# T in two tiles of long runs, an unsigned read, a moved weight piece and turns on the sync queue: the prologue of a Fourier and SoLU kernel

## The chip, the cores and the metric

The kernel runs on one core of one Trainium2 chip. The metric is the device time of one execution in microseconds. "Span" is the length of the profiled execution; the device time is some 2 us longer.

## The reference

```python
X = np.fft.fft(x, axis=1)                 # x: (8, 3136, 256) float32
X = np.fft.fft(X, axis=2).real            # -> (25088, 256) tokens
h = X @ w_in                              # w_in (256, 1024)
e = np.exp(h - h.max(-1, keepdims=True))
solu = h * (e / (e.sum(-1, keepdims=True) + 1e-9))
ln = (solu - mean(solu)) / sqrt(var(solu) + 1e-6) * g_ln
return ln @ w_out                         # w_out (1024, 256)
```

The weights come as 64-bit floats, in two 32-bit words each, and the kernel makes float32 of them.

## The kernel before

The sequence transform is done in two factors. The first (F) runs chunk by chunk and its results go out to a DRAM tile `zd`; a **turn** reads them back with another order of axes (`g`); the second factor is a product with the table `T`, one per **unit** of 128 rows, and there are 100 units in four pairs. Each unit then goes through `up` (the product with w_in, TensorE), `even` and `join` (VectorE), `expo` (ScalarE), `product` (VectorE), a mean (GpSimd), `square` (ScalarE) and, four steps later, `down` (the product with w_out). `ev`, which `even` writes, is the first VectorE step of a unit, and serves below as the mark of where a unit stands.

```python
T = const.tile([P, NK, P], FP32, name="T")

def turn(pr, i, engines=(nc.gpsimd,) * 4):               # four transfers of 160 KB
    pr.g[i] = gpool.tile([P, KG, D], FP32, tag="g", name="g")
    for j in range(4):
        engines[j].dma_start(out=pr.g[i][j * NH : (j + 1) * NH, :, :], in_=zd[j, :, i * KG : (i + 1) * KG, :])

def spread(t):                                           # r: one row of q across partitions
    nc.sync.dma_start(out=t.r, in_=t.q[0:1, P : 2 * P])

def load_table(self):                                    # T, two loads of 400 KB, runs of 256 B
    for b in range(2):
        r = slice(b * N2, (b + 1) * N2)
        nc.sync.dma_start(out=T[r, :, r], in_=t_tab)

# narrow(): two 32-bit words to one float32
bits(lo, lo, 1, ALU.logical_shift_right)
m = lo.bitcast(FP32)
nc.vector.scalar_tensor_tensor(out=m, in0=lo, scalar=2.0 ** -31, in1=mantissa, op0=ALU.mult, op1=ALU.add)

def centre(self):                                        # takes the mean of w_out's rows off
    for c in range(KF):
        nc.tensor.matmul(cs, ones, Wo[:, c, :], start=(c == 0), stop=(c == KF - 1))
    nc.scalar.mul(out=wbar, in_=cs, mul=1.0 / FF)
    nc.vector.tensor_tensor(out=Wo, in0=Wo, in1=wbar...., op=ALU.subtract)

# ... chunks of the first pair; w_out and T are loaded behind chunk 3 ...
turn(first, 0, (nc.sync, nc.gpsimd) * 2)
...                                                      # narrow_out(0..3)
for i in range(len(units) + lag):                        # the train, one unit a step
    ...
    even(cur, up(cur, 0)); odd = up(cur, 1)
    take2(nxt, transform2(pairs[nxt.p], nxt.k1)); spread(nxt)
    ...
    join(cur, odd); ...; expo(cur); ...
    for s in cur.signs: product(cur, s)                  # GpSimd's mean (nmean) right behind each
    if i == 0: weights.centre()
    for s in cur.signs: square(cur, s)
    ...
    if 0 < i + 1 < NK // KG: turn(first, i + 1)          # turns 1 to 4, by GpSimd
    if ahd: ahead(ahd, cur.k1)                           # loads and gathers of the next pair
```

## Time and profile before

| | before |
|---|---|
| device time, median of 3 | 1192.98 us (1190.93 to 1195.39) |
| span of the profiled run | 1189.9 us |
| ev of units 0, 1, 2, 3 | 63.15, 71.33, 78.19, 87.04 us |
| first matmul of unit 5's `up` | 101.25 us |
| last ScalarE scaling starts | 1186.42 us, 3.48 us ahead of the end |

Units 0 to 4 are the start; behind them TensorE is full, and each unit takes 11.65 us. What the start wins or loses moves everything behind it.

These are the rows of the program's last line (engine, operation, count, then shortest, median and longest duration in ns, and the first and last time), and below it the waits of the sync engine from 1160 us on (total, times, longest us):

```profile
L722 POOLq DRAIN  x3: 46/102/3455, 1183.5 to 1189.6; - x3
```

### The profile page before, as it was taken

To read this page: it belongs to the slowest core of one execution; us is meant where nothing else is said; L and a number is where in the kernel's file an instruction comes from. 1 tells how busy PE (TensorE), PEld (TensorE's weight loads), DVE (VectorE), ACT (ScalarE), POOL (GpSimd) and SP (SyncE) were. 2 spreads that over 40 slices of the span, in tenths; PEclk is the share of its full clock that TensorE was granted. 3 is DMA by queue.
4 is the path that set the end of the run, shared out by engine and by line. 5 is a ranking of instruction groups with operands and counts; after the bars stand their busy time and mean duration, and the time that the engine had idled before them with its cause. 6 is when DMAs were issued, how large, how long until landed. Compare 5 with 4: busy or idle time off the path is not lost. (4 is left out here: it accounts for less than half of the span.)

```text
span 1189.9 us, 15918 instructions
## 1 busy us (share of the span) xinstructions
PE 1154.2 (97%) x4720; PEld 875.9 (74%) x4720; DVE 907.9 (76%) x1241; ACT 679.0 (57%) x1404; POOL 496.9 (42%) x964
## 2 busy tenths in 40 slices
PE   2889999999999999999999999999999999999998
PEld 1556777777777777777777777777777777777787
DVE  8879777777768877787778878777786887877780
ACT  4557655655546656565555656565555555655561
POOL 3045444443544443432544453433453344333433
PEclk9999999999999999999999999999999999999999
DMA  9873765756775765654775776664684453544534
GB/s 246 206 187 72 190 162 152 200 140 163 171 172 160 187 172 155 167 144 131 172 187 159 176 177 154 158 181 122 150 198 131 109 152 100 145 111 120 142 92 117
DMA packets 460886, 185.39 MB, mean 156 GB/s; under 512 B 428854, under 2 KB 442750, under 8 KB 460800
## 3 DMA queue, kind: packets, MB, share of 16 engines
q1 hardware_dynamic: 446848, 145.63, 48.6%
q0 software_dynamic: 13952, 38.75, 11.9%
q8 instruction: 38, 0.62, 0.2%
q14 instruction: 48, 0.39, 0.1%
HBM read 44.78 MB, written 38.80 MB: 70 GB/s over the span
## 5 line engine op out<-in xcount | busy, mean ns | idle before, releaser
L323 PE MATMUL ps_o<-Wo,uT 128*128 128x256 f32 x3136 | 693.4, 379 | 0.3 <-ACT ot L328 0.3
L323 PEld LDWEIGHTS ps_o<-Wo,uT 128*128 128x128 f32 x3136 | 611.0, 196 | 62.8 <-issue 0.9
L222 PE MATMUL ps_h<-Wi,q 128*128 128x512 f32 x800 | 362.3, 595 | 0.1
L254 DVE SCALAR_TENSOR_TENSOR u<-h,u 128x1024 f32<-128x1024 f32 x196 | 240.1, 1225 | 57.0 <-ACT u L246 31.1
L236 DVE CUSTOM_DVE_ANT_0 h<-ev,ps_h 128x1024 f32<-128x1024 f32 x196 | 231.8, 1219 | 50.3 <-PE ps_h L222 41.3
L256 POOL TENSOR_SCALAR nmean<-usum 128x1 f32<-128x1 f32 x196 | 80.4, 411 | 445.7 <-DVE u L254 445.5
L222 PEld LDWEIGHTS ps_h<-Wi,q 128*128 128x128 f32 x800 | 152.7, 191 | 149.8 <-issue 144.6
L263 ACT ACTIVATE h<-u,nmean 128x1024 f32<-128x1024 f32 x196 | 225.0, 1149 | 61.3 <-POOL nmean L256 60.0
L228 DVE SCALAR_TENSOR_TENSOR ev<-w_mid,r,ps_h 128x1024 f32<-128x1024 f32 x100 | 127.8, 1278 | 133.1 <-PE ps_h L222 126.2
L246 ACT ACTIVATE u<-h,neg 128x1024 f32<-128x1024 f32 x196 | 225.4, 1150 | 6.5
L291 DVE STREAM_TRANSPOSE v<-u 128x1024 f32<-128x1024 f32 x192 | 228.6, 1236 | 0.1
L200 ACT COPY q<-ps 128x256 f32<-128x256 f32 x100 | 37.2, 372 | 289.3 <-PE ps L194 263.0
L328 ACT ACTIVATE ot<-ps_o,rs 128x256 f32<-128x256 f32 x196 | 87.0, 462 | 61.3 <-PE ps_o L323 55.2
L335 POOL DMA_INDIRECT out_dram<-ot,idx x96 | 103.0, 1073 | 35.4 <-issue 20.7
L194 PEld LDWEIGHTS ps<-T,g 128*128 128x128 f32 x400 | 60.9, 194 | 52.1 <-issue 50.9
L169 PE MATMUL ps<-y,F 98*100 98x258 f32 (+3 forms) x288 | 72.2, 387 | 22.2 <-DVE y L122 22.2
L278 POOL TENSOR_TENSOR rs<-v,neg_half 128x2 f32<-128x2 f32 (+1 forms) x100 | 84.2, 842 | 7.8
L244 ACT ACTIVATE neg<-nmax 128x1 f32<-128x1 f32 x196 | 38.3, 195 | 61.0 <-DVE nmax L236 60.2
L169 PEld LDWEIGHTS ps<-y,F 98*100 98x100 f32 x288 | 46.0, 179 | 34.6 <-DVE y L122 20.9
L275 POOL TENSOR_SCALAR v<-ssq 128x2 f32<-128x2 f32 (+1 forms) x100 | 23.3, 233 | 112.7 <-ACT h L263 112.7
L194 PE MATMUL ps<-T,g 128*128 128x128 f32 x400 | 61.5, 277 | 4.4 <-DMA g<-zd 4.4
L184 POOL DMA_DIRECT2D g<-zd x78 | 46.7, 608 | 36.6 <-DMA zd<-z_g 30.5
(74 smaller groups left out, 464.7 us busy)
## 6 DMA issues: line engine op xcount, KB each, us to landing
uT<-v SPq DMA_DIRECT2D x752, 128.0 KB
out_dram<-ot SPq DMA_DIRECT2D x100, 128.0 KB
g<-zd POOLq DMA_DIRECT2D x78, 160.0 KB, 4.2
xa<-in_x_dram SPq DMA_DIRECT2D x28, 392.0 KB
zd<-z SPq DMA_DIRECT2D x24, 400.0 KB
raw_in<-in_moe_w_in_dram SPq DMA_DIRECT2D x4, 512.0 KB
raw_out<-in_moe_w_out_dram SPq DMA_DIRECT2D x2, 1024.0 KB
r<-q SPq DMA_DIRECT2D x100, 0.5 KB
```

The costliest lines, as they stand in the source:

```text
L169: nc.tensor.matmul(o[..., cs], F[:, 2 * t + h, :], i[..., cs], start=first, stop=True, skip_group_check=True)
L194: nc.tensor.matmul(ps[:, h * P : (h + 1) * P], g[:, k, h * P : (h + 1) * P], T[:, k1, :], start=(h == 0), stop=True, skip_group_check=True)
L222: nc.tensor.matmul(ps[:, fs], t.q[:, c * P : (c + 1) * P], Wi[:, c, fs], start=True, stop=True)
L228: nc.vector.scalar_tensor_tensor(out=t.ev, in0=w_mid, scalar=t.r, in1=ps, op0=ALU.mult, op1=ALU.add)
L236: nc.vector.tensor_tensor_reduce(out=t.h[s], in0=t.ev, in1=ps, scale=1.0, scalar=-3.0e38, op0=ALU.subtract if s else ALU.add, op1=ALU.max, ...
L246: nc.scalar.activation(out=t.u[s], in_=t.h[s], func=ACT.Exp, bias=t.neg[:, s : s + 1], accum_out=t.esum[:, s : s + 1])
L254: nc.vector.scalar_tensor_tensor(out=t.u[s], in0=t.h[s], scalar=1.0, in1=t.u[s], op0=ALU.mult, op1=ALU.mult, accum_out=t.usum[:, s : s + 1])
L263: nc.scalar.activation(out=t.h[s], in_=t.u[s], func=ACT.Square, bias=t.nmean[:, s : s + 1], accum_out=t.ssq[:, s : s + 1])
L291: nc.vector.transpose(out=t.batch.v[:, t.w, :, o], in_=t.u[s])
L323: nc.tensor.matmul(ps, uT[:, c, :, s], Wo[:, c, :], start=(c == 0), stop=(c == KF - 1))
L328: nc.scalar.mul(out=t.ot[s], in_=ps, mul=t.rs[:, s : s + 1])
L335: dma = nc.gpsimd.indirect_dma_start(out=out, out_offset=bass.IndirectOffsetOnAxis(ap=idx[:, i : i + 1], axis=0), in_=t.ot[s], in_offset=None)
```

## The change

The intent was to have turn 0 in SBUF earlier, by short issues of T ahead of it; to take eight shifts off VectorE; to keep the last piece of w_out and the centring off the path of unit 0; and to free GpSimd from the issues of turns 1 to 4.

```diff
-    T = const.tile([P, NK, P], FP32, name="T")
+    T = [const.tile([P, 2, n, N2], FP32, name=f"T{n}") for n in (KG, NK - KG)]
 ...
-        bits(lo, lo, 1, ALU.logical_shift_right)
-        nc.vector.scalar_tensor_tensor(out=m, in0=lo, scalar=2.0 ** -31, in1=mantissa, ...)
+        nc.vector.scalar_tensor_tensor(out=m, in0=lo.bitcast(U32), scalar=2.0 ** -32, in1=mantissa, ...)
 ...
-        def load_table(self):
+        def load_table(self, i):
+            k1 = slice(KG, NK) if i else slice(0, KG)
             for b in range(2):
-                r = slice(b * N2, (b + 1) * N2)
-                nc.sync.dma_start(out=T[r, :, r], in_=t_tab)
+                nc.sync.dma_start(out=T[i][b * N2 : (b + 1) * N2, b], in_=t_tab[:, k1, :])
 ...
-                weights.load_table()
+                weights.load_table(0)
 ...
         turn(first, 0, (nc.sync, nc.gpsimd) * 2)
+        weights.load_table(1)
 ...                            # narrow_out(3) from ahead of unit 0 to unit 0's step
-                if i == 0:
+                if i == 1:
                     weights.centre()
 ...
-                turn(first, i + 1)
+                turn(first, i + 1, (nc.sync,) * 4)
```

More of the change, by code (lines that the diff above doesn't have):

```diff
@@ L11 @@
 I32 = mybir.dt.int32
+U32 = mybir.dt.uint32
 ALU = mybir.AluOpType
@@ L191, in transform2 @@
         g = pr.g[i]
+        table = T[0][:, :, k, :] if i == 0 else T[1][:, :, k1 - KG, :]
         ps = ps_m.tile([P, KD * P], FP32, tag="m", name="ps2")
         for h in range(KD):
-            nc.tensor.matmul(ps[:, h * P : (h + 1) * P], g[:, k, h * P : (h + 1) * P], T[:, k1, :],
+            o = ps[:, h * P : (h + 1) * P].rearrange("p (b k) -> p b k", b=2)
+            nc.tensor.matmul(o, g[:, k, h * P : (h + 1) * P], table,
                              start=(h == 0), stop=True, skip_group_check=True)
@@ L394, in narrow @@
         bits(mantissa, hi, 0xFFFFF, ALU.bitwise_and, 0x100000, ALU.bitwise_or)
-        bits(lo, lo, 1, ALU.logical_shift_right)
         m = lo.bitcast(FP32)
-        nc.vector.scalar_tensor_tensor(out=m, in0=lo, scalar=2.0 ** -31, in1=mantissa, op0=ALU.mult, op1=ALU.add)
+        nc.vector.scalar_tensor_tensor(out=m, in0=lo.bitcast(U32), scalar=2.0 ** -32, in1=mantissa, op0=ALU.mult,
+                                       op1=ALU.add)
         nc.vector.scalar_tensor_tensor(out=unit, in0=hi, scalar=top_bit, in1=unit, op0=ALU.bitwise_and,
@@ L543 @@
             nc.vector.memset(limits[:, i : i + 1], limit)
-        nc.vector.memset(T, 0.0)
+        for t in T:
+            nc.vector.memset(t, 0.0)
         weights.exponent_in(0)
@@ L581 @@
         weights.exponent_out(3)
-        confine(weights.units[-1])
         weights.product_in(2)
-        for i in range(1, 4):
+        for i in range(1, 3):
             weights.narrow_out(i)
@@ L590 @@
             spread(t)
+        confine(weights.units[-1])
         for c in (2, 3, 0, 1, 4, 5, 6, 7):
@@ L626 @@
                 ps_o = [down(old, s) for s in order]
+            if i == 0:
+                weights.narrow_out(3)
             if cur:
```

## The prediction

> **What bounds the kernel now.** I read the page's 40 slices first, then the busy time by stretches, then the timeline of each engine over the first 110 us.
>
> ```profile
> PE   2889999999999999999999999999999999999998
> PEclk9999999999999999999999999999999999999999
> ```
>
> TensorE is at nine tenths or more from slice 4 on; only slices 1 to 3 (the first 90 us) and the very last have room. The stretches confirm it (columns: window, its length, then busy us of each engine, clock, DMA share, GB/s):
>
> ```profile
> 75.00:83.00 8.00, 4.72 (x26) 3.39 (x26) 6.05 (x10) 5.52 (x12) 5.27 (x12) 0.97 0.89 210
> 300.00:600.00 300.00, 300.00 (x1237) 229.42 (x1236) 232.96 (x310) 175.02 (x367) 134.60 (x263) 1.00 0.65 166
> ```
>
> TensorE is busy 300.00 of 300 us in the middle (and 190.00 of 190 before it), so from about 105 us the kernel is a rigid TensorE-bound train: one unit each 11.65 us (the L323 groups of the timeline start at 128.44, 140.09, 151.74). None of that is touched. A change in the first 100 us moves the whole train by what it saves before the train starts, and the most there is to win is the idle and half-speed TensorE time between about 54 and 98 us. The TensorE timeline there (start, duration, then the idle time before it and its releaser):
>
> ```profile
> 50.54 3.60 PE L454 MATMUL wps<-w_in,w_mid 128*128 128x512 f32 x8
> 58.54 1.99 PE L194 MATMUL ps<-T,g 128*128 128x128 f32 x8 [4.40 <-DMA g<-zd]
> 60.32 4.45 PE L222 MATMUL ps_h<-Wi,q 128*128 128x512 f32 x8
> 64.61 0.61 PE L194 MATMUL ps<-T,g 128*128 128x128 f32 x4
> 65.05 3.62 PE L484 MATMUL cs<-Wo,ones 128*128 128x256 f32 x16
> ...
> 82.14 0.82 PE L303 MATMUL ps_t<-ident,u 128*128 128x128 f32 x4 [3.15 <-ACT q L200]
> 82.75 5.17 PE L222 MATMUL ps_h<-Wi,q 128*128 128x512 f32 x8
> ```
>
> Two holes, 4.40 and 3.15 us, each followed by slow matmuls: the same eight records of L222 take 4.45 and 5.17 us instead of 3.60. Hole one is the first turn (read back from DRAM). Its cause is in the sync queue's timeline:
>
> ```profile
> 37.50 5.39 SPq L440 DMA_DIRECT2D T<-in_t_tab_dram x1
> 43.00 5.04 SPq L177 DMA_DIRECT2D zd<-z_u x1
> 48.14 1.04 SPq L177 DMA_DIRECT2D zd<-z_g x3
> 53.72 0.81 SPq L184 DMA_DIRECT2D g<-zd x2
> ```
>
> The two loads of T (400 KB each) hold the queue from 36.77 to 42.89, and the write of piece 3 behind them until 48.04. The last writes of zd are issued by 49.77 and the turn is released at 53.72, although ScalarE had its last copy out at 47.89. In the stretches, DMA moved 403 GB/s at 38.5 to 41.25 us (w_out) but 141, 147 and 128 GB/s from 44 to 52.25: short packets of T.
>
> **What the Trainium skill says.** "DMA: Bandwidth & Descriptors", section Specifications, wants at least 512 B per descriptor for line rate, and its section "Why small descriptors are slow" works out 11 cycles for a 256 B descriptor where 8 carry data. T's runs are 64 floats, 256 B; the trace agrees, and is worse (about 140 against 403 GB/s). The same page, "SWDGE vs HWDGE vs iDMA", says that the descriptors of GpSimd's transfers are computed by software on GpSimd. The trace: each turn piece occupies GpSimd for 0.577 us or more, four of them 2.4 us. "TensorE: Matmul & The Clock Gate", Part 1, gives half the clock after about 3.4 us of idling; the granted clock of 57.75 to 60.50 was 0.65, and the slow matmuls above agree. On the conversion of unsigned words I found nothing that gives a cost.
>
> **The change, part by part.**
>
> 1. T in long runs, first tile first. Packets go from 3,200 of 256 B (25 runs x 64 rows x 2) to 128 runs of 1,280 B before the first turn (160 KB) and 128 of 5,120 B after it. The first tile should take well under 1 us. The writes of pieces 3 to 6 then go when their copies are done, and the last at about 48.1 instead of 49.8, with an almost idle DMA. I estimate 2 us to land, so the turn is released near 50.3 instead of 53.7. From release to TensorE took 4.8 us (53.72 to 58.54, the GpSimd-issued half last), so g could be there at 55.1; the second tile of T (640 KB) now shares the DMA with it and I add 0.4: 55.5. TensorE reaches this point at 54.1 as before, because the stage ahead of it is gated by a DMA (VectorE waits 2.37 us for room until 34.08) and nothing takes bytes out ahead of that. Hole one: 4.40 to about 1.4 us, gain 3.0. A hole of 1.4 us should not cool the clock: eight L194 take 1.22 instead of 1.99 and L222 3.6 instead of 4.45, gain 1.6. So the first VectorE step of unit 0, at 63.15 now, comes at about 58.6 (-4.5).
>
> 2. Low words unsigned. Eight shifts of 128x512 go, 0.42 us each, 0.34 start to start: 2.7 us of VectorE. The four of w_in lie ahead of the DMA wait at 34.08: worth 0. The four of w_out shorten the run that ends at 60.87 now; three of them (1.0) bring narrow piece 2 from 57.8 to 56.8 or earlier, which keeps VectorE off the path of 58.6. By themselves they would not move the end.
>
> 3. Last piece of w_out after unit 0's join, and the centring one step later. VectorE would have been busy to about 59.5 with piece 3; moved, it costs 2.6 us (0.34+0.61+0.78+0.88) between join and product, where VectorE waits 1.54 us for the exponential now. The 3.62 us of cs matmuls and the 2.29 us subtraction move from step 0 to step 1; same work. From 58 to 98 us VectorE sets the pace (14.28 of 15 us busy at 83 to 98), so I follow it, with the durations of the timeline. Unit 0: ev 58.6, h 60.3 to 61.5, piece 3 to 64.2, u 65.4 (now 68.8). Unit 1: ev 65.4, two h to 69.1, two u to 72.3, the second held by ScalarE's exponential (now 78.2). Subtraction to 74.6.
>
> 4. Turns 1 to 4 from the sync queue. GpSimd now spends 74.05 to 79.1 on four turn issues and two gathers, so nmean of unit 1, ready to compute at 76.9, runs at 79.14; ScalarE's squares wait 2.45 us, and TensorE's hole two follows. After the change the gathers are issued near 73, nmean runs at once, the squares end near 74 and hole two shrinks to the VectorE pace. Unit 2: ev 74.6, h 75.9 to 78.2 without the 1.26 us wait of now, copies 79.5, u 81.9; unit 3's ev at **81.9 instead of 87.04**. From there both kernels have the same order and the same 7.2 us per step until the train: **-5.1 us**. The matmul through T now reads two runs of 64 columns; L169 reads runs of 129 with a step and still costs about what L323 does per column, so I give it nothing.
>
> Sum: 1192.98 - 5.1 = **1187.9 us**.
>
> **The rivals.** (a) *The second tile of T takes the place of the first.* It is queued before the GpSimd-issued half of the turn has run, 640 KB against 320 KB. If they share evenly, g comes about 1.5 us later than I take it: 1189.5. For it: the landing of turns varied from 3.1 to 5.6 us. (b) *VectorE as bound.* If piece 3 and the subtraction push out units 0 to 2 by more than the waits they fill, or uint32 input is slower than int32, up to 2 us of the 5 are given back: 1190. Against: an unsigned word leaves the count of elements as it is. (c) *The sync queue blocks.* It is in order; turn 1 waits for all eight large zd writes, and the r of units 3 to 6 now stand behind turns. Turn 1 was released at 74.05; r of unit 3 is needed near 82, so there are some 6 us of slack. If it failed, TensorE would stall again: 1193 to 1196. (d) *All of it hits*: g lands before TensorE asks (54.2) and hole one vanishes: 6.4 us, 1186.5. (e) *Hidden anyway*: if the last zd copy rather than T sets the release, part 1 loses half its worth: 1190.
>
> **Range and chances.** The terms give 3 to 6.5 us; the runs of before spread 4.5 us (1190.93 to 1195.39), so a median of three can be off by 1.5. Range 1184.0 to 1191.5. Two per cent is 24 us: more than all the TensorE idle time after 54 us, so faster by over 2% 0.01, within 2% 0.98, slower by over 2% 0.01 (only a blocked queue or a slower matmul through T, 400 records in the train, could do it).
>
> **What would show it.** T's issues short and the first zd writes leaving by 39 us; the release of the turn at 50 to 51 instead of 53.72; L194's first idle 1 to 2 us and L222 after it near 3.6; ev of unit 0 at 58 to 59.5; nmean of unit 1 right behind its product, and no 3.15 us hole; the train's starts 4 to 6 us earlier and still 11.65 apart. A step other than 11.65, r landing late, or L397 over 0.8 us would prove me wrong.

## More of the kernel before

```profile
SPq L722 <- DMA out_dram<-ot: 1.2, 1, 1.2
SPq L722 <- PEq L722: 0.7, 2, 0.5
```

GpSimd's own queue (POOLq) ends with a drain of 3,455 ns, and the barrier at the end (where the engines wait for each other) costs the sync engine 0.5 us at most. The three drains of that row don't follow each other at once: the long one is the first. It starts at 1183.5, so it ends near 1187.0, while the sync engine has the last store behind it only at 1189.0. The drain has some 2 us to spare: by this reckoning a drain that is longer by up to 2 us costs nothing here.

## The result, and the profile after

The changed kernel took **1196.48 us** (median of 4, 1196.35 to 1196.92); the runs of the kernel before, 1193.62 (median of 4). The ratio is 1.0027, with a 95% interval of 1.0007 to 1.0046. A ratio here is the mean time of one kernel's runs over that of the other's in the same rounds, so it is not quite the ratio of the medians. Two repeats, on two chips, gave 1.0043 (1.0029 to 1.0057) and 1.0029 (1.0015 to 1.0043): by these means the change makes the kernel 3 to 5 us slower. All of this is within 2%. The predicted range ended at 1191.5.

The start first. This is TensorE's timeline of the changed kernel (start, duration, then the idle time before it and its releaser):

```profile
51.58 3.60 PE L458 MATMUL wps<-w_in,w_mid 128*128 128x512 f32 x8
59.22 2.05 PE L198 MATMUL ps<-T,g 128*128 128x128 f32 x8 [4.04 <-issue]
61.06 5.41 PE L226 MATMUL ps_h<-Wi,q 128*128 128x512 f32 x8
...
82.31 0.66 PE L307 MATMUL ps_t<-ident,u 128*128 128x128 f32 x4 [0.92 <-ACT q L204]
82.80 3.63 PE L226 MATMUL ps_h<-Wi,q 128*128 128x512 f32 x8
...
90.67 0.66 PE L307 MATMUL ps_t<-ident,u 128*128 128x128 f32 x4 [2.02 <-ACT q L204]
91.16 5.29 PE L226 MATMUL ps_h<-Wi,q 128*128 128x512 f32 x8
```

Hole one is 4.04 us where it was 4.40, and the eight matmuls behind it take 5.41 us where they took 4.45. Hole two is 0.92 where it was 3.15, as wanted; but a hole of 2.02 us stands a unit later, and the matmuls behind that one are slow. The sync queue's timeline shows what became of turn 0:

```profile
38.47 1.22 SPq L444 DMA_DIRECT2D T<-in_t_tab_dram  x2
...
50.90 0.80 SPq L186 DMA_DIRECT2D g<-zd  x2
51.75 1.11 SPq L444 DMA_DIRECT2D T<-in_t_tab_dram  x2
```

T's first tile is issued in 1.22 us (6.12 before), and the turn is released at 50.90 (53.72 before; 50.3 was predicted). From there to TensorE it took 8.32 us, where it had taken 4.82. Between them stand the second tile's two loads. VectorE's timeline of the first steps of units 0 to 3:

```profile
64.78 1.28 DVE L232 SCALAR_TENSOR_TENSOR ev<-w_mid,r,ps_h 128x1024 f32<-128x1024 f32 x1 [7.60 <-PE ps_h L226]
71.45 1.28 DVE L232 SCALAR_TENSOR_TENSOR ev<-w_mid,r,ps_h 128x1024 f32<-128x1024 f32 x1
80.57 1.28 DVE L232 SCALAR_TENSOR_TENSOR ev<-w_mid,r,ps_h 128x1024 f32<-128x1024 f32 x1
88.46 1.28 DVE L232 SCALAR_TENSOR_TENSOR ev<-w_mid,r,ps_h 128x1024 f32<-128x1024 f32 x1 [0.59 <-DMA r<-q]
```

Unit 3 stands at 88.46 where 81.9 was predicted and 87.04 was before, and it waited 0.59 us for its r. From there both kernels run at the same pace; the matmuls of unit 5 start at 102.67 (101.25 before). The middle of the train is as full as before (busy us of 300, the columns as in the prediction's stretches):

```profile
300.00:600.00 300.00, 300.00 (x1236) 229.00 (x1235) 232.35 (x309) 174.63 (x369) 134.35 (x263) 1.00 0.64 165
```

So the start accounts for +1.42 us of the +4.5 us of span in this pair of profiles, and 1.04 us of it was there before turn 0 (the matmuls with w_mid start at 51.58, and at 50.54 before). The rest is behind the train. The last scaling starts at 1187.25, 0.83 us later than before, but the span ends 7.15 us behind it, not 3.48. The same two views of the end as above, after:

```profile
L731 POOLq DRAIN  x3: 46/102/9282, 1184.3 to 1194.1; - x3
```

```profile
SPq L731 <- PEq L731: 4.4, 2, 3.9
SPq L731 <- DMA out_dram<-ot: 1.1, 1, 1.1
```

GpSimd's last drain takes 9,282 ns instead of 3,455, and the sync engine now stands 3.9 us in the barrier at the end. The program's last store was in memory (the sync engine has it behind it at 1189.8); only GpSimd was still draining, from 1184.3 to 1193.6. The drain grew by 5.8 us, the 2 us to spare are used up first, and 3.7 us show.

**Theory.** Three things ate the gain and more: (A) the second tile of T shares the DMA with turn 0 and delays it, by some 3.5 us in this profile; (B) r of unit 3 stands behind turn 1 in the sync queue; (C) GpSimd's last drain is 5.8 us longer, because GpSimd issues sixteen transfers fewer, and 3.7 us of it show. **Rivals**: that the start of the DMA (the wait for room that ended at 34.08 before and at 35.55 after) or the drain vary from run to run; that the drain hangs on GpSimd's instructions, or on the other parts of the change.

### The profile page after: what moved, and what is told of

It reads as the page before. It is cut to its first block, busy times and chain, and to the rows that moved or that the text cites. A ratio compares the mean times of both kernels' runs of the same rounds, so it can differ in the third digit from the quotient of the medians. Undisturbed runs are those within 1.5% of the kernel's fastest.

```text
span 1194.4 us, 15910 instructions
## 1 busy us (share of the span) xinstructions
PE 1154.8 (97%) x4720; PEld 875.7 (73%) x4720; DVE 904.9 (76%) x1234; ACT 678.6 (57%) x1404; POOL 487.1 (41%) x948
## 3 DMA queue, kind: packets, MB, share of 16 engines
q0 software_dynamic: 12928, 36.12, 11.0%
## 4 chain that ended last, share of the span: by engine, by line
PE 93%; DMA 4%; DVE 1%; ACT 1%; issue 1%; POOL 0%; SPq 0%; DVEq 0%; ACTq 0%
PE ps_o L327 57%; PE ps_h L226 28%; PE ps L171 4%; PE ps L198 4%; DMA room<-in_x_dram 2%; DMA r<-q 1%; DMA T<-in_t_tab_dram 0%; DMA raw_in<-in_moe_w_in_dram 0%; PE wps L458 0%; DVE h L240 0%; ACT u L250 0%; DVE u L258 0%; DMA zd<-z_g 0%; ACT h L267 0%; POOL nmean L260 0%
## 5 line engine op out<-in xcount | busy, mean ns | idle before, releaser
L260 POOL TENSOR_SCALAR nmean<-usum 128x1 f32<-128x1 f32 x196 | 83.5, 426 | 459.9 <-DVE u L258 459.8
L339 POOL DMA_INDIRECT out_dram<-ot,idx x96 | 103.1, 1074 | 36.9 <-issue 22.6
L198 PEld LDWEIGHTS ps<-T,g 128*128 128x128 f32 x400 | 60.9, 194 | 51.7 <-issue 50.8
L171 PE MATMUL ps<-y,F 98*100 98x258 f32 (+3 forms) x288 | 71.5, 384 | 24.0 <-DVE y L124 23.3
L198 PE MATMUL ps<-T,g 128*128 128x128 f32 x400 | 61.6, 278 | 4.0 <-issue 4.0
L131 POOL TENSOR_TENSOR xa<-xa,xb 98x1020 f32<-98x1020 f32 (+1 forms) x24 | 54.5, 2271 | 0.0
```

Source lines behind the costliest of these rows:

```text
L171: nc.tensor.matmul(o[..., cs], F[:, 2 * t + h, :], i[..., cs], start=first, stop=True, skip_group_check=True)
L198: nc.tensor.matmul(o, g[:, k, h * P : (h + 1) * P], table, start=(h == 0), stop=True, skip_group_check=True)
L339: dma = nc.gpsimd.indirect_dma_start(out=out, out_offset=bass.IndirectOffsetOnAxis(ap=idx[:, i : i + 1], axis=0), in_=t.ot[s], in_offset=None)
```

## The experiments

All gave right results. "Before" in a ratio is the kernel before on the same chip, as a rule in the same rounds (for e4 and e8, 11 of its 12 runs are those that e3's ratio rests on). One table first, from the profile of each run. "Early mark" is the start of the last early product (the eight matmuls of L454 or L458 with w_mid), ahead of turn 0 in all of them; "unit 3" is its ev counted from that mark; "tail" is from the start of the last ScalarE scaling to the end of the span.

| run | median us | ratio (95%) | early mark | unit 3 behind it | tail | last drain ns |
|---|---|---|---|---|---|---|
| before, first profile | 1193.62 | 1 | 50.54 | 36.5 | 3.5 | 3,455 |
| before_again | 1192.79 | 1.0021 (1.0001 to 1.0042) | 53.78 | 35.0 | 3.4 | 3,457 |
| after, first profile | 1196.48 | 1.0027 (1.0007 to 1.0046) | 51.58 | 36.9 | 7.2 | 9,282 |
| after_again | 1195.94 | 1.0043 (1.0029 to 1.0057) | 51.44 | 35.1 | 7.2 | 9,285 |
| after_third | 1194.80 | 1.0029 (1.0015 to 1.0043) | 51.91 | 34.1 | 7.1 | 9,282 |
| e1_table_late | 1193.78 | 1.0019 (1.0006 to 1.0033) | 52.37 | 35.1 | 7.1 | 9,282 |
| e2_turns_gpsimd | 1192.38 | 1.0007 (0.9993 to 1.0020) | 51.26 | 35.8 | 3.4 | 3,450 |
| e12_late_and_gpsimd | 1191.23 | 0.9986 (0.9971 to 1.0001) | 52.68 | 34.7 | 3.4 | 3,442 |
| e5_sync_alone | 1197.11 | 1.0038 (1.0020 to 1.0056) | 53.99 | 35.5 | 7.1 | 9,282 |
| e6_table_alone | 1192.49 | 0.9998 (0.9983 to 1.0014) | 52.79 | 35.5 | 3.4 | 3,444 |
| e10_turn4_back | 1190.63 | 0.9991 (0.9978 to 1.0004) | 50.62 | 35.6 | 3.1 | 3,020 |
| e3_turn1_sync | 1187.86 | 0.9952 (0.9935 to 0.9970) | 51.01 | 31.4 | 3.1 | 3,316 |
| e3_again | 1187.82 | 0.9964 (0.9935 to 0.9993) | 51.91 | 31.2 | 3.1 | 3,314 |
| e4_prefetch_later | 1191.51 | 0.9993 (0.9974 to 1.0011) | 51.23 | 31.2 | 3.1 | 3,317 |
| e8_subtract_moved | 1190.13 | 0.9978 (0.9960 to 0.9996) | 51.22 | 30.9 | 3.1 | 3,313 |
| e9_alternate | 1188.73 | 0.9965 (0.9944 to 0.9985) | 51.12 | 30.8 | 3.4 | 3,199 |

**before_again and after_again: both kernels once more, no edit.**

> The kernel before, unchanged, for a second profile on the chip on which the others of this call run. It is to tell what differs from chip to chip or run to run. Two readings of the first two profiles are open. If the start of the DMA (VectorE's wait for the room of a chunk ended at 34.08 us before and 35.55 after) and the last drain of GpSimd (3,455 ns before, 9,282 ns after) belong to the kernels, this run shows 34.1 and about 3.5 us again, and the train (first step of unit 3 at 87.0) where it was. If they belong to the chip or the run, they come out elsewhere. Time: ratio 1.000 to before, within 0.003.

> The changed kernel, unchanged, on the same chip as the others. Theory (the start is chance, the second tile of T and the drain are the kernel's): the wait for room ends within 0.5 us of that of the kernel before in this call; the turn is released near 50 us and its readback lands 8 us later (it took 8.2); the first step of unit 3 comes within 1 us of that of before instead of 5 us ahead; GpSimd's last drain is near 9.3 us; ratio 1.002 to 1.004. Rival (drain and start both chance of the run): drain near 3.5 us and a ratio of 1.000 or below.

The same kernel came out at 1.0021 of itself, and its early mark lay 3.2 us later than in the first profile. So the first 50 us vary from run to run, by more than the effects in question: the rival is right about the start, and positions of single profiles are to be compared from the early mark on. A ratio off by 0.2% proves nothing alone. The drain did not vary: 3,457 and 9,285 ns. It belongs to the kernel.

**e1_table_late: the changed kernel with T's second tile behind the first reads of turn 0.**

```diff
         turn(first, 0, (nc.sync, nc.gpsimd) * 2)
-        weights.load_table(1)
 ...
         for t in units[:2]:
             take2(t, transform2(pairs[0], t.k1))
             spread(t)
+        weights.load_table(1)
```

> The changed kernel with the load of T's second tile (640 KB) moved behind the first two reads of turn 0, so that it can't share the DMA with the half of the turn that GpSimd issues. Theory (the second tile took the place of the first): the readback of turn 0 lands 4.5 to 5 us after its release instead of 8.2, TensorE's hole before the first matmul through T falls from 4.04 us to 1 or less, the eight records behind it take 3.6 us instead of 5.4, the first VectorE step of unit 0 comes 4 to 5 us earlier than in the changed kernel, the one of unit 3 some 3 to 5 us earlier, and the time is 3 to 5 us below the changed kernel: ratio to before 0.999 to 0.9995 with the long drain still there. Rival (the late start of the DMA, or GpSimd's own slowness in issuing its half, sets the landing): no change, ratio as the changed kernel.

TensorE's timeline, then VectorE's row of unit 3:

```profile
56.34 1.13 PE L198 MATMUL ps<-T,g 128*128 128x128 f32 x8 [0.38 <-issue]
57.49 3.70 PE L226 MATMUL ps_h<-Wi,q 128*128 128x512 f32 x8
```

```profile
87.50 1.28 DVE L232 SCALAR_TENSOR_TENSOR ev<-w_mid,r,ps_h 128x1024 f32<-128x1024 f32 x1 [3.69 <-DMA r<-q]
```

Theory A is shown for turn 0: from the release at 51.68 to TensorE 4.66 us instead of 8.32 (7.12 in after_again, 6.96 in after_third), a hole of 0.38 instead of 4.04, and matmuls at full speed. The landings, by the semaphores in the trace, say the same: the two pieces that GpSimd issues land 3.3 us after their issue before and in e1, and 5.1 and 5.4 us after it in e10 below, which has the tile early. TensorE does not wait for the tile itself: in the changed kernel the last piece of `g` lands at 59.03, TensorE starts at 59.22, and the tile's second load lands at 59.39. Unit 0 came at 59.58, where the prediction had 58.6. The Trainium skill, "DMA: Bandwidth & Descriptors", section "Queues, rings and completion order", says that each DMA engine goes round the queues that have work, packet by packet; this agrees with a tile in the sync queue that holds up the half of the turn in GpSimd's queue, though no run here shows single packets taking turns. But the early gain was gone by unit 3, which waited 3.69 us for r. The expected 3 to 5 us at unit 3 did not come; counted from the mark it stood at 35.1, as in after_again. The saved time only turned into a new wait, and the ratio, 1.0019, missed the expected 0.999 to 0.9995.

**e2_turns_gpsimd: the changed kernel with turns 1 to 4 back on GpSimd; e12: that and the late tile.**

```diff
-                turn(first, i + 1, (nc.sync,) * 4)
+                turn(first, i + 1)
```

> The changed kernel with turns 1 to 4 issued by the sync and GpSimd queues in turn, as before; the rest of the change stays. Theory (GpSimd's last drain depends on how many transfers it issued): the last drain is 3.5 us again and the end comes 3 to 4 us earlier relative to the train than in the changed kernel; the read-in of r for unit 3 no longer stands behind turn 1; ratio to before 0.998 to 1.001, unless hole two (3.15 us before) comes back and takes 1 to 3 us of it. Rival (the drain varies by itself, or with the length of the program): drain 9 us here too, and a ratio at or above the changed kernel's.

> Both edits at once: T's second tile behind the first reads of turn 0, and turns 1 to 4 issued by GpSimd as before. (The record of the run with the turns alone says 'in turn'; GpSimd issued all sixteen pieces before, and does so here.) Theory (two independent losses in the changed kernel, the shared DMA at turn 0 and the long last drain of GpSimd): the first step of unit 0 near 59.6 us and of unit 2 near 76.5 (measured with the first edit), 8.8 us more to unit 3 (measured with the second), so unit 3 near 85.4; last drain 3.45 us; 1.5 to 2 us under the run with the second edit alone, and 1 to 2 under the kernel before: ratio 0.998 to 1.0. Rival (hole two, back again, eats what the early start gives): unit 3 at 87 and a ratio of 1.001.

The drain was 3,450 ns again, the tail 3.4 us, and the ratio fell from 1.0043 to 1.0007: theory C holds here. In e12 unit 0 came at 60.01 and unit 2 at 76.89, but unit 3 at 87.34, not 85.4, because hole two was back, and larger: TensorE stood 4.76 us at 82.45. GpSimd's timeline of e12 shows why:

```profile
74.40 2.39 POOL L186 DMA_DIRECT2D g<-zd  x4 [3.70 <-DMA r<-q]
77.09 1.07 POOL L111 DMA_INDIRECT xb<-in_x_dram,idx  x1 [0.30 <-issue]
78.46 0.96 POOL L111 DMA_INDIRECT xb<-in_x_dram,idx  x1 [0.30 <-issue]
79.45 0.46 POOL L260 TENSOR_SCALAR nmean<-usum 128x1 f32<-128x1 f32 x2
```

GpSimd stands 3.70 us until turn 1's data is out (the page names r's landing, at 74.36, as the releaser; but the long wait in GpSimd's queue, 3,557 ns, ends with the landing of the last piece of `zd`, at 73.69), issues turn 1, then issues two gathers, and only then takes the two means for which ScalarE's squares wait. An earlier unit 0 only makes it stand longer. So the rival took its share, and e12's ratio (0.9986) leaves open whether it beats the kernel before.

**e5_sync_alone and e6_table_alone: one part each on the kernel before** (turns 1 to 4 on the sync queue; T in two tiles, the second late).

> The kernel before with one part of the change alone: turns 1 to 4 on the sync queue. Theory: GpSimd's last drain takes 9.28 us instead of 3.45, which puts the end 3.5 to 4 us later relative to the train; the hole of 3.15 us before the products of unit 2 goes or shrinks, because the four issues no longer stand ahead of GpSimd's mean of unit 1; r of unit 3 lands late behind turn 1; the train moves by -1 to +1 us, and the ratio is 1.002 to 1.004. Rival (the drain comes from T's tiles or from the order of the weights): 3.45 us here and a ratio of 0.998 to 1.0.

> The kernel before with one part alone: T in two tiles of long runs, the second loaded behind the first reads of turn 0. The shifts, piece 3 and the centring stay where they were. Theory: the turn is released 3 us earlier and lands near 55.5; the hole before the first product through T falls below 1.5 us; but VectorE is busy with piece 3 until 60.9 us, so the first step of unit 0 comes at 61 rather than at 59.6, 2 us ahead of before, and the train 1.5 to 2 us ahead; drain 3.45 us; ratio 0.998 to 0.9995. Rival (the hole was not T's): first step at 63, ratio 1.000.

The turns alone bring the long drain (9,282 ns), a wait of 2.57 us for r at unit 3, and 1.0038. The tile alone takes hole one to 0.53 us and unit 0 to 61.65, as worked out for a VectorE that is busy with piece 3 until then; yet its ratio is 0.9998, because hole two grew to 4.52 us (at 83.42): GpSimd took unit 1's means at 80.41, behind turn 1 and two gathers as in e12, and so kept what the tile gave. Neither part pays alone.

**e3_turn1_sync and its repeat: late tile, turn 1 on the sync queue behind r, turns 2 to 4 by GpSimd.**

```diff
             take2(nxt, transform2(pairs[nxt.p], nxt.k1)); spread(nxt)
+            if i == 1:
+                turn(first, 1, (nc.sync,) * 4)
 ...
-            if 0 < i + 1 < NK // KG:
-                turn(first, i + 1, (nc.sync,) * 4)
+            if 1 < i + 1 < NK // KG:
+                turn(first, i + 1)
```

> T's second tile late; turn 1 alone on the sync queue, and there behind the read-in of r of the same step; turns 2 to 4 by GpSimd. Twelve transfers of turns by GpSimd, four fewer than before, twelve more than the changed kernel. Theory for the train: no wait for r (3.69 us with the tile late, 1.02 in the changed kernel), so unit 3 comes 7.3 to 8.5 us behind unit 2: near 84 to 85. For the last drain three theories: it grows with the number of GpSimd transfers that are missing (5.83 us for 16, so 3.45 + 1.46 = 4.9 us here); it is a step (3.45 or 9.28 and nothing between); or it hangs on which queue issued turns 2 to 4 last (3.45). Ratio 0.997 to 1.0.

> The version with T's second tile late, turn 1 on the sync queue behind r and turns 2 to 4 by GpSimd, unchanged, in the same call as the other candidate, because it had the best ratio (0.9952, 0.9935 to 0.9970) although its profile shows a hole of 3.5 us that the later version did not have. If that ratio was the version's own: 0.9945 to 0.996 again. If it was the luck of six runs (its runs spread from 1184.8 to 1189.2): 0.997 to 0.999.

This is the version that beats both kernels: 0.9952 and, on another chip, 0.9964. Unit 3 came at 82.38 us, 31.4 behind the mark, with no wait for r (issued at 71.12 instead of 77.47): theory B is shown, and the place that the prediction gave (81.9) was reached. The drain was 3,316 ns, not 4.9 us: its length does not grow with each missing transfer. What is left is TensorE's next hole:

```profile
85.08 1.19 PE L198 MATMUL ps<-T,g 128*128 128x128 f32 x4 [3.54 <-ACT h L267]
86.06 3.62 PE L307 MATMUL ps_t<-ident,u 128*128 128x128 f32 x16
89.47 4.33 PE L226 MATMUL ps_h<-Wi,q 128*128 128x512 f32 x8
```

The page names ScalarE as the releaser, but L198 is the first product of unit 5, which needs turn 1; its four pieces had been issued at 72.31 to 74.4, and in the trace they have landed at 82.69, 83.41, 84.17 and 84.83, with two loads and two gathers of the next pair in flight beside them. In e3_again, where the same hole is 2.64 us at 84.86, the page does name the landing of `g`.

**e4_prefetch_later and e8_subtract_moved: the next pair's first loads two steps later; and the centring's subtraction behind the first VectorE step of unit 2.**

> The version with T's second tile late, turn 1 on the sync queue behind r, turns 2 to 4 by GpSimd, and one more move: the first two loads of the next pair (2 x 392 KB and two gathers) go out in the step of unit 2 instead of unit 0. In the version without this move turn 1 was issued at 72.3 to 74.4 us but landed at 80.5 to 83.9, behind those loads, and TensorE stood 3.54 us at 85.08 for it; unit 4 came 10.2 us behind unit 3 instead of 7.2. Theory (those loads took turn 1's share of the DMA): turn 1 lands 4 to 6 us after its issue, no hole at 85, unit 4 7.2 us behind unit 3, train 2 to 3 us earlier, ratio 0.992 to 0.994. Rival (turn 1 is slow in itself on the sync queue, whose keep writes are still in flight): no change, 0.995.

> As the run before it in this call, with the subtraction of the centring (2.29 us of VectorE, two inputs in SBUF) moved from right behind the products of unit 1 to behind the first step of unit 2, where VectorE waits for TensorE's second half. In the changed kernel GpSimd's two means of unit 1 take 2.77 us together while that subtraction runs, against 0.45 when it does not. Theory (a two-input VectorE operation keeps GpSimd from its operands): the two means take under 1.6 us; ScalarE's second square of unit 1 starts some 2 us earlier; unit 2's first step 2.3 us earlier; unit 3's 0 to 1.5 us earlier; ratio 0.001 lower at most. Rival (the second mean waits for its input from VectorE): 2.8 us as before.

In e4's profile turn 1 had landed at 76.85 (84.83 in e3), which is what the theory of the shared DMA asks for; TensorE's wait for it was gone, and unit 4 came 7.8 us behind unit 3 (10.2 in e3). Another hole, of 2.03 us, now stood at 85.35, with slow matmuls behind it (5.29 us), as in the changed kernel. But its five further runs took 1188.96 to 1193.69, and the ratio was 0.9993: worse than e3 on the same chip. Why is not settled. The gathers now stand, behind turn 3, ahead of GpSimd's means of unit 3 (a hole of 1.55 us at 94.44), and in e8's profile the same hole was 3.24 us and left sixteen matmuls at 6.18 us instead of 3.73; that the timed runs of e4 met this is likely, but no profile of them exists.

e8 tests the means. In the changed kernel GpSimd's two means of unit 1 took 2.78 us while VectorE subtracted (78.36 to 80.65):

```profile
77.94 2.78 POOL L260 TENSOR_SCALAR nmean<-usum 128x1 f32<-128x1 f32 x2
```

In e8 VectorE's subtraction ran from 74.17 to 76.46. GpSimd's timeline:

```profile
71.78 0.23 POOL L260 TENSOR_SCALAR nmean<-usum 128x1 f32<-128x1 f32 x1 [2.79 <-DVE u L258]
73.14 0.21 POOL L260 TENSOR_SCALAR nmean<-usum 128x1 f32<-128x1 f32 x1 [1.13 <-DVE u L258]
...
74.71 1.83 POOL L279 TENSOR_SCALAR v<-ssq 128x2 f32<-128x2 f32 x1 [0.81 <-ACT h L267]
```

The means take 0.23 and 0.21 us, and the operation that now meets the subtraction takes 1.83 us and ends with it. The Trainium skill, "SBUF — State Buffer", section "SBUF: two separate sides", says that a VectorE operation with two inputs in SBUF and a GpSimd operation that reads SBUF exclude each other for a whole instruction; the trace agrees, with 1.83 us for an operation of 0.23. Unit 2 came 2.3 us earlier (72.97) than in e4, but unit 3 only 0.3 us, as VectorE does the same work; e8's ratio (0.9978) is not clearly apart from e4's.

**e9_alternate: e8 with turns 1 and 3 on the sync queue, 2 and 4 by GpSimd.**

```diff
-            if i == 1:
-                turn(first, 1, (nc.sync,) * 4)
+            if i in (1, 3):
+                turn(first, i, (nc.sync,) * 4)
 ...
-            if 1 < i + 1 < NK // KG:
+            if i + 1 in (2, 4):
                 turn(first, i + 1)
```

> As the version with the later prefetch and the moved subtraction, with turns 1 and 3 on the sync queue (each behind r of its step) and turns 2 and 4 by GpSimd: eight transfers fewer than before. In the version without it, GpSimd issued turn 3 (2.4 us) and two gathers (2.7 us) ahead of its means of unit 3, which came at 91.13 though unit 3's products were ready near 89; TensorE stood 3.24 us at 94.11 and cooled, and the train began 2.6 us late. Theory: with turn 3 off GpSimd the means of unit 3 come by 89.5, the hole at 94 goes under 1 us, no half-speed matmuls before the train, and the train starts near 98 (matmuls of unit 5) instead of 101: ratio 0.993 to 0.996, drain 3.2 us. Rival (VectorE sets the pace there and the hole is only its shadow): the train at 99 to 101, ratio 0.996 to 0.998.

The hole at 94 became one of 1.94 us at 92.59, not under 1, and the sixteen matmuls behind it were still slow (5.36 us). Unit 5's matmuls started at 98.32 (101.04 in e8), so most of the loss was GpSimd's queue, and the train came where the theory had it (near 98). Part of the hole that is left is GpSimd's queue too: its two gathers end at 89.27, and the first of the means, whose input VectorE had ready at 88.43, starts at 89.30. The ratio, 0.9965, is as good as e3's, with runs closer together (1188.04 to 1190.11).

**d1, d2 and d3: the drain by itself** (single runs, state unknown; only the drain is read). d1 and d3 are the kernel before with turns 3 and 4, or 2 to 4, on the sync queue; d2 is the changed kernel with four GpSimd memsets of a scratch column at each of turns 1 to 4.

> The kernel before with turns 3 and 4 (eight transfers) on the sync queue, for the length of GpSimd's last drain alone. Sixteen transfers fewer gave 9.28 us, four fewer 3.32, none fewer 3.44 to 3.46. If it grows step by step past some count: a value between 3.3 and 9.3. If it is a step between two lengths: 3.2 to 3.5 or 9.3. Time: within 0.3% of before in the first case of the step, 3.5 us above it in the second.

> The changed kernel with four small GpSimd memsets of a scratch column added at each of the turns 1 to 4, so that GpSimd has as many instructions as before but sixteen transfers fewer. If the last drain hangs on the number of GpSimd's transfers (or packets of its queue, 12,928 against 13,952), it stays at 9.28 us. If it hangs on the number of GpSimd's instructions, so on where in its program the end falls, it goes to about 3.45 us.

> The kernel before with turns 2 to 4 (twelve transfers) on the sync queue, for the length of GpSimd's last drain. Measured so far: 16 fewer 9.28, 8 fewer 3.21, 4 fewer 3.32, none fewer 3.44 to 3.46 us (queue packets 12,928, 13,440, 13,696 and 13,952). It falls by 0.1 us per four transfers until a jump of 6.2 us. If the jump lies at 12 to 16 fewer: 3.1 us here. If it lies at 8 to 12: 9.35 to 9.45 us, and the lengths above the jump fall by 0.1 us too.

| GpSimd transfers fewer | packets of its queue | last drain ns | runs |
|---|---|---|---|
| 0 | 13,952 | 3,442 to 3,457 | before, before_again, e2, e12, e6 |
| 4 | 13,696 | 3,313 to 3,317 | e3, e3_again, e4, e8 |
| 8 | 13,440 | 3,199 and 3,211 | d1, e9 |
| 12 | 13,184 | 3,020 and 3,029 | d3, e10 |
| 16 | 12,928 | 9,282 to 9,285 | after (three), e1, e5, d2 |

The row of d2, with as many GpSimd instructions as before:

```profile
L734 POOLq DRAIN  x3: 46/102/9285, 1184.8 to 1194.6; - x3
```

So the drain hangs on the number of GpSimd's transfers (or of their packets: the two go together in all these runs), not on its instructions, and not on which of the turns are moved (d3 moves turns 2 to 4, e10 turns 1 to 3). It falls a little with each four transfers, and jumps by 6.3 us between twelve and sixteen fewer. What makes the jump, and where it comes again, stays open.

**e10_turn4_back: the changed kernel with turn 4 alone given back to GpSimd, beside the changed kernel.**

```diff
-                turn(first, i + 1, (nc.sync,) * 4)
+                turn(first, i + 1, (nc.gpsimd if i == 3 else nc.sync,) * 4)
```

> The changed kernel with one edit: turn 4 (four transfers, near 89 to 99 us) goes back to GpSimd; turn 0 with T's second tile and turns 1 to 3 stay as in the changed kernel. Queue packets 13,184 as in the run with twelve transfers fewer, whose last drain was 3.03 us. Theory (the number of GpSimd's transfers alone sets the last drain, and the drain alone is what the changed kernel loses at its end): the drain is 3.0 us, the time is 3.5 to 4.5 us under the unchanged changed kernel of this call, ratio to before 0.999 to 1.001 while the other stays at 1.002 to 1.004. Rival (the drain hangs on other things too, or the barrier at the end waits for something else by then): drain 9.28, or drain 3.0 and less than 2 us won.

> The changed kernel once more, unchanged, beside the version with turn 4 given back, so that the two are compared on one chip: ratio to before 1.002 to 1.005, drain 9.28 us.

```profile
L731 POOLq DRAIN  x3: 46/102/3020, 1183.4 to 1188.1; - x3
```

```profile
SPq L731 <- PEq L731: 0.7, 2, 0.5
```

Giving back four transfers of sixteen took the drain to 3,020 ns, the barrier to 0.5 us and the median from 1194.80 to 1190.63: 4.2 us, as much as the tail shrank (7.1 to 3.1). The ratios are 0.9991 and 1.0029. Turn 0 with T's second tile was left as it was (the turn took 6.9 us from release to TensorE). So the long drain is what made the changed kernel slower: without it, it is about equal to the kernel before (0.9991, interval 0.9978 to 1.0004). The predicted gain is missing there too; e1 and e3 show where it went.

## Why the prediction was wrong

It said 1187.9 us and 1184.0 to 1191.5; the kernel took 1194.8 to 1196.5 in three rounds. By its own steps:

- **What bounds the kernel, and that only the start matters: wrong by omission.** The sum, 1192.98 - 5.1, took the end of the program as a constant. It held neither a term for GpSimd's last drain nor a rival that touched the end. The drain grew by 5.8 us, of which 3.7 us show in the span (7.15 - 3.48), and giving back four transfers won 4.2 us. But this is only one half of the miss of 8.6 us (1196.48 against 1187.9): without it (e10) the kernel was about equal to before, where 5.1 us of gain were predicted. The other half is in part 1 and in the slack of rival (c).
- **Part 1, the release of the turn: right.** Predicted 50.3, measured 50.90 with a start that was 1.5 us late.
- **Part 1, "the second tile of T (640 KB) now shares the DMA with it and I add 0.4": this term failed.** Measured, 8.32 us from release to TensorE instead of 4.82, so 3.5 us (2.1 to 2.3 us in after_again, after_third and e10); with the tile late (e1), 4.66. Rival (a) named the mechanism, and with 1.5 us was also too small. This is where the predicted gain went: 4.5 of the 5.1 us were to come by unit 0's first step, at 58.6. It came at 64.78 (62.49 and 63.10 in the repeats, 63.15 before). The walk from there to unit 3 was right: 23.3 us predicted, 23.68 measured with 0.59 of waiting for r.
- **Part 1, no cooling (1.6 us): failed with it.** The hole stayed at 4.04 us and the matmuls took 5.41 us. In e1, with a hole of 0.38, they took 3.70. A hole of the predicted 1.4 us was never met at this place. Unit 0's 58.6 was met at 59.58 in e1.
- **Part 2, the shifts worth 0: consistent, but not isolated.** The unsigned read costs what the signed one did (712 and 693 ns as means for the two weights, 712 and 692 before).
- **Part 3, piece 3 between join and product: right.** It ran there from 67.66 to 70.30 us, 2.64 us, where 2.6 was predicted.
- **Part 4, hole two and unit 3 at 81.9: half right.** Hole two shrank from 3.15 to 0.92 us. But the second mean did not "run at once": it met the subtraction that part 3 had moved there (the pair took 2.78 us). And rival (c), r behind the turns, which the text gave some 6 us of slack, did happen: r of unit 3 was issued at 77.47 instead of 72.98, and unit 3 waited for it, 0.59 to 2.57 us in five of the six profiles that have turn 1 on the sync queue ahead of that r and no late tile (none in after_third), and 3.69 with the tile late. What failed there is the time to land: the text left r some 6 us between its issue and its use, and in the changed kernel it landed at 88.36, 10.9 us after its issue, behind turn 1 and two loads in its queue. With both repaired (e3) unit 3 came at 82.38 and the time was 1187.86 and 1187.82 us: the predicted size was there to be won, but by another order of transfers than the changed kernel's, so that this number is no merit of the prediction.
- **Range and chances.** The chance of 0.98 for "within 2%" was right. The range of 7.5 us was too narrow for a sum of terms that all pointed one way, on a kernel whose own start varies by over 3 us.

## What to carry to other kernels

When transfers move from one queue to another, look at both ends of the program too: an engine's last drain and the barrier behind it are part of the time, and GpSimd's drain depended here on how many transfers it had issued. A load that is moved out of the way of a transfer must also be moved past its landing, not only past its issue, and small loads that the next step waits for belong ahead of bulk ones in an in-order queue. Undo one part at a time, and compare profiles from a mark that lies behind the part that varies by chance; several waits in a row hide each other, and here no part paid until the next wait behind it was taken away as well.

## What the Trainium skill lacked or had wrong

- No page that I read says that GpSimd's drain at the end of a program depends on how many transfers it issued. The runs show 3,442 to 3,457 ns with 13,952 packets in its queue, 3,020 to 3,029 with 13,184 and 9,282 to 9,285 with 12,928. It would belong to "DMA: Bandwidth & Descriptors".
- "DMA: Bandwidth & Descriptors", section "SWDGE vs HWDGE vs iDMA", sends plain transfers to the sync or ScalarE queue; the runs show a case where with sixteen of them moved there the end of the program was longer, and four given back to GpSimd won 4.2 us (e10 against after_third), so that a rule without that cost is incomplete.
- "TensorE: Matmul & The Clock Gate", Part 1, puts the cold clock after about 3.4 us without activity. Here idle stretches of 2.02 us were followed by matmuls at 5.29 us instead of 3.60, while one of 2.85 us (d2) was not followed by any slow ones (1.13 and 3.70 us). That the window runs freely, as the same part says, could let the longer stretch pass; it does not explain that 2.02 us were enough, if a whole window has to be idle. The runs do not show the window itself.
